# A two-layer attention and token-MLP kernel: odd columns of w2 packed and kept in DRAM, and fill work placed anew

## The chip, the core and the metric

The kernel runs on one core of a Trainium2 chip, in one launch. The metric is the device time of that launch in microseconds (us); the median of three runs before the change is 1305.59 us (1304.1 to 1305.82). All weights and activations are bf16 in DRAM; products accumulate in fp32 in PSUM.

## The reference, cut to what matters

`x` is 2048 positions by 1024 features. Two layers follow each other with the same weights:

```python
x = x + A(layernorm(x), wqkv, wo)      # attention over 8 positions at distance 2, 32 heads of 32
x = x + B(layernorm(x), w1, b1, w2, b2)
x = x + A(...)
x = x + B(...)

# A: q, k, v = x @ wqkv; position s attends to s, s-2, ..., s-14; then @ wo
# B mixes positions, not features (2048 positions -> 3584 -> 2048 positions):
h = layernorm(x)
u = gelu(einsum("bsd,sf->bdf", h, w1) + b1)
y = einsum("bdf,fs->bds", u, w2) + b2       # transposed back to positions x features
```

Because attention goes in steps of two, even positions never see odd ones inside A. In B all positions mix.

## The kernel before, in words

**Classes.** The positions are split by parity into class 0 (even) and class 1 (odd), 1024 positions each, in eight tiles of 128 positions. Attention runs class by class. In the MLP, a tile of output positions of class c needs every other column of w2: columns `c::2` of a block of 256 (`DIL` is 2).

**Stages of a layer.**

1. Attention (`Attn.stream`). TensorE projects q, k and v (L410). VectorE multiplies q with shifted k (L442), and TensorE adds those products up to scores with a selection matrix (L447). Softmax follows on VectorE and ScalarE (L453 to L468). The probabilities go to DRAM and come back spread over partitions (`pd`, `pb`, on POOL's queue), and VectorE multiplies and adds them with v (L503 to L509). Each class has two groups `n` of heads, so `n` runs from 0 to 3.
2. Output projection of a class (`out_proj`, L629). VectorE empties the PSUM banks and adds the residual (L650 or L653), the row goes to DRAM (`xa`), and a layernorm gives `h2`.
3. First MLP product (`gemm1`, L680), over 14 blocks `fb` of 256 columns of w1. For blocks below `NPART` the two classes are done apart: class 0's partial product is copied to `g` (L686), and later class 1's is added to it (L691) and goes through gelu (L692). For the others both classes accumulate in one bank, and gelu reads it (L688).
4. Second MLP product (`gemm2_tile`, L704), tile by tile: 28 blocks of w2 rows times two halves of the features. VectorE adds bias and residual (L709), the row goes to DRAM (`xb`), and in layer 0 a layernorm and a DMA transpose (L234) give the input `hT` of the next layer's attention.

**What runs inside what.** VectorE's attention work leaves TensorE idle, so other work is woven in as fill. `weave` takes a lead (attention and then class 1's output projection) and named fills, and keeps two clocks of its own, `pe` and `dve`, moved on by costs written beside each piece. When a lead piece must wait until some time, `reach` pulls fill pieces until `pe` is there. The fills are `second` (in layer 0 class 1's normalization; in layer 1 class 1's second MLP product of layer 0, the "class-1 pass"), `v_ahead` (class 1's v), `out0` (class 0's output projection), `partials` (class 0's first MLP product, blocks 0 to 5) and `late` (blocks 6 to `NPART`, whose `g` buffers hold class 1's v until attention is past them). Beside that, `weave` pulls a piece of `out0` each time lead work of `OUT0_GAP` has gone by on VectorE. Class 1's output projection begins with three row tiles at once, six banks without their last two contraction steps; the planner places it by `("less", "oT", -6.0)`, that is, 6 us by its own clock after the last attention piece.

After the weave come the blocks from `NPART` on for both classes, then blocks 0 to `NPART` for class 1, and then the second MLP product. In layer 0 only class 0's half of it runs here (the "class-0 pass"); the class-1 pass is woven into layer 1's attention. In layer 1 both classes run here, from the same w2 tiles. The order of instructions on each engine is then settled by the framework's scheduler.

**Queues and buffers.** SP's queue issues, in order, all loads of weights and rows and the transposes. POOL's issues stores and the probabilities. `wbp` is a pool of five slots for w1, w2, wo and v-weight tiles; a load waits on SP until TensorE is done with a slot, and what stands behind it on SP waits too. `w2_tiles` loads a block of 256 columns in four tiles of seven row blocks. `x2p` has four slots for rows (`xr`), normalized rows (`hb`) and `tmp`. `psp` has six PSUM banks. `tpl` has two slots, tag `T`, used by attention.

Of the kernel before, what the change touches and what calls it, by code (L numbers as in the profile page):

```python
# [13 lines left out]
BF16 = mybir.dt.bfloat16  # L14

P = 128
# [3 lines left out]
DIL = 2  # L20
# [6 lines left out]
def kernel(  # L27
# [32 lines left out]
    FB = 256  # L60
    NFB = F // FB
    GF = FB // P
    NPART = 10
    NW2 = 4
    HF = FT // NW2
    SLACK = 0.5
    PB_LAG = 12.0
    PDW = 4 * SB * W * TB + 512
    OUT0_GAP = 7.0
    assert D == H * DH and W == 8 and SC == 1024 and HD * KD == H and SB * CH == 32  # L70
    scale = float(DH) ** -0.5

# [97 lines left out]

    xa = [[dram.tile([SC, D], BF16, name=f"xa{li}{c}") for c in range(DIL)] for li in range(2)]
    xb = [dram.tile([SC, D], BF16, name=f"xb{c}") for c in range(DIL)]
    pd = [dram.tile([CH, PDW], BF16, name=f"pd{n}") for n in range(2 * DIL * NCQ)]

    xin_v = x_in.rearrange("(i m c) d -> c i m d", m=P, c=DIL)
# [433 lines left out]
    def out_proj(at_, c, res, dst, h2, on_act):  # L609

        early = 0 if on_act else 3
        if early:
            yield "pe", 1.28 * early * NDC, [("oT", 0), ("less", "oT", -6.0)], [], 0.0
        dst_v = rows(dst)
        wo_t = [[None, None] for _ in range(NDC)]
        for n in range(NDC):
            for hf in range(2):
                wt = wb("wo", [P, KD // 2, 512])
                nc.sync.dma_start(out=wt[:], in_=wo_v[hf, :, :, n * 512:(n + 1) * 512])
                wo_t[n][hf] = wt  # L620
        for hf in range(2):
            h2[c][hf] = hx(f"h2{c}{hf}", [P, NT // 2, D])
        banks = {}

        def multiply(i, n, kts):
            if (i, n) not in banks:
                banks[(i, n)] = bank()
            for kt in kts:
                nc.tensor.matmul(banks[(i, n)][:], lhsT=at_.oT[c][kt][:, i * P:(i + 1) * P],  # L629
                                 rhs=wo_t[n][kt // 4][:, kt % 4, :], start=(kt == 0), stop=(kt == KD - 1))  # L630

        def kts(i):
            return range(KD - 2 if i < early else 0, KD)

        for i in range(early):
            for n in range(NDC):
                multiply(i, n, range(KD - 2))
        xrs = Rows([res[i] for i in range(NT)], 2)
        for i in range(NT):
            if early:  # L640
                yield "pe", 0.43 * len(kts(i)), ["oT"], [], 3.6
                on_act = i % 2 == 0
            xn = xrs.take()
            s1 = st("s1", [P, NDC]) if on_act else None
            for n in range(NDC):
                cols = slice(n * 512, (n + 1) * 512)
                multiply(i, n, kts(i))
                ps = banks.pop((i, n))
                if on_act:
                    nc.vector.scalar_tensor_tensor(out=xn[:, cols], in0=ps[:], scalar=1.0, in1=xn[:, cols], op0=ALU.mult,  # L650
                                                   op1=ALU.add, accum_out=s1[:, n:n + 1])
                else:
                    nc.vector.tensor_tensor(out=xn[:, cols], in0=ps[:], in1=xn[:, cols], op=ALU.add)  # L653
            nc.gpsimd.dma_start(out=dst_v[i], in_=xn[:])
            h = h2[c][i // 4][:, i % 4, :]
            if on_act:
                nm, rs = stats_act(xn[:], 1.0 + EPS, eps2, h, s1)
                norm_act(h, xn[:], nm, rs)
            else:
                mean, rs = stats_dve(xn[:], 1.0 + EPS, eps2)  # L660
                norm_dve(h, xn[:], mean, rs)
            if not early:
                yield 3.5, 0.0
# [31 lines left out]
    def gemm2_tile(c, i, w2t, xs, dst, hT, on_act=False, end=False):  # L695
        xo = xs.take()
        halves = [slice(n * 512, (n + 1) * 512) for n in range(NDC)]
        groups = [halves[:1], [slice(512, 768)], [slice(768, 1024)]] if end else [halves]
        for cols in groups:
            acc = [bank() for _ in cols]  # L700
            for n in range(NW2):
                for ft in range(n * HF, (n + 1) * HF):
                    for ps, xc in zip(acc, cols):
                        nc.tensor.matmul(ps[:, 0:xc.stop - xc.start], lhsT=w2t[n][:, ft % HF, c::DIL],  # L704
                                         rhs=g[ft // GF][:, ft % GF, xc], start=(ft == 0), stop=(ft == FT - 1))
                if n < NW2 - 1:
                    yield 1.5 * len(cols), 0.0
            for ps, xc in zip(acc, cols):
                nc.vector.scalar_tensor_tensor(out=xo[:, xc], in0=ps[:, 0:xc.stop - xc.start], scalar=b2_sb[:, i, c:c + 1],  # L709
                                               in1=xo[:, xc], op0=ALU.add, op1=ALU.add)  # L710
            yield 1.5 * len(cols), 0.75 * len(cols)
            if end:
                nc.sync.dma_start(out=dst[:, cols[0]], in_=xo[:, cols[0]])
        if not end:
            nc.gpsimd.dma_start(out=dst, in_=xo[:])
        if hT is None:
            return
        hb = x2("hb")
        if on_act:
            nm, rs = stats_act(xo[:], 1.0, eps1, hb[:])  # L720
            norm_act(hb[:], xo[:], nm, rs)
        else:
            mean, rs = stats_dve(xo[:], 1.0, eps1)
            norm_dve(hb[:], xo[:], mean, rs)
        to_hT(hb[:], hT, c, i)
        yield 0.0, 0.0 if on_act else 2.0

    def w2_tiles(i):
        tiles = []
        for n in range(NW2):  # L730
            t = wb("w2", [P, HF, FB])
            nc.sync.dma_start(out=t[:], in_=w2_v[:, n * HF:(n + 1) * HF, i * FB:(i + 1) * FB])
            tiles.append(t)
        return tiles

    def run(*its):
        for _ in chain(*its):
            pass

    def weave(lead, fills, lags):  # L740
# [35 lines left out]
        for kind, *unit in lead:  # L776
            if kind == "open":
                after = {"out0": "oT", "partials": "out0", "late": "out0", "v_ahead": "second"}.get(unit[0])
                opened[unit[0]] = when.get(after, float("inf")) if after else pe
            elif kind == "drain":  # L780
                while unit[0] in opened:
                    pull(True)
            elif kind == "at":
                pe, dve = unit
            elif kind == "pe":
                cost, waits, sets, then = unit
                reach(ready(pe, waits))
                pe += cost
                when.update((x, pe + 2.0) for x in sets)
                if then:  # L790
                    dve = max(dve, pe) + then
            else:
                cost, waits, sets, lag, then = unit
                dve = ready(dve, waits) + cost
                if then:
                    reach(dve)
                    pe += then
                when.update((x, dve + lag) for x in sets)
                if list(opened)[:1] == ["out0"] and opened["out0"] < pe:
                    due += cost  # L800
                    if due > OUT0_GAP:
                        due -= OUT0_GAP
                        pull()
        while pull(True):
# [4 lines left out]
    for li in range(2):  # L809
# [22 lines left out]
        def second_class():  # L832
            new_hT(hT, 1)
            xs = Rows([rows(xa[0][1])[i] for i in range(NT)], 1)
            for i in range(NT):
                if first:
                    prologue_tile(1, i, hT)
                    yield 0.0, 2.0 * (i % 2 == 0)
                else:
                    yield from gemm2_tile(1, i, w2_tiles(i), xs, xb[1][i * P:(i + 1) * P, :], hT, on_act=i < NT - 2)  # L840

        def v_ahead():
            if not first:
# [18 lines left out]
        if first:  # L862
            with at(top):
                ln_exp_table()
            hT = [[None, None] for _ in range(DIL)]
            new_hT(hT, 0)
            xs = Rows([rows(xa[0][0])[i] for i in range(NT)], 1)
            for i in range(NT):
                run(gemm2_tile(0, i, w2_tiles(i), xs, xb[0][i * P:(i + 1) * P, :], hT))
        else:  # L870
            xs = Rows([rows(xa[1][c])[i] for i in range(NT) for c in range(DIL)], 1)
            for i in range(NT):
                w2t = w2_tiles(i)
                for c in range(DIL):
                    run(gemm2_tile(c, i, w2t, xs, out_v[c, i], None, end=(i == NT - 1 and c == DIL - 1)))
# [30 lines left out]
```

## Time and profile before

| | before |
|---|---|
| median of three runs | 1305.59 us |
| profiled execution, time | 1303.7 us |
| profiled execution, span | 1301.9 us |
| TensorE busy | 1274.3 us (98%) |
| VectorE busy | 669.5 us (51%) |
| ScalarE busy | 463.9 us (36%) |
| mean granted TensorE clock | 0.997 |
| DMA moved | 173.00 MB, mean 133 GB/s |

The span is the time from the first to the last instruction of the profiled execution. In a line of a timeline the columns are start, duration, engine, source line, operation, and what is written from what; in brackets stands the idle time before it and what ended that. In a line of waits they are the waiting instruction, what released it, the total, how often, and the longest.

Where the stages lie in the span, by TensorE's timeline: layer 0's attention and fills up to 288.8 us, class 1's output projection to 323.5, first MLP product to 464.5, class-0 pass to 561.2; layer 1's attention, with the class-1 pass from 575 to 758.7, then fills up to 925.5, output projection to 953.3, first MLP product to 1105, second to the end.

### The profile page before, as it was taken

Reading aid. Unit: us, or ns where it says so; the run is one execution under the profiler, and the core shown is the slowest. Engines: PE = TensorE matmul, PEld = TensorE weight load, DVE = VectorE, ACT = ScalarE, POOL = GpSimd, SP = SyncE. Lnnn points to the kernel's source line nnn. Section 1 sums busy time; section 2 is a strip of 40 time slices with the busy share of each in tenths; the row PEclk is TensorE's granted clock in tenths of the full one; section 3 lists DMA queues with packets and bytes.
Section 4 is the critical chain, followed back from the end, with each engine's and each line's share of the span. In section 5 each row is a group of like instructions: output and inputs, shape, how many; then the busy total and the mean of one; then the engine's idle time right before and its main releaser. Section 6 shows DMA issues by size and latency. Waiting matters only on the chain. (4 is left out here: it accounts for less than half of the span.)

```text
span 1301.9 us, 15529 instructions
## 1 busy us (share of the span) xinstructions
PE 1274.3 (98%) x6284; PEld 575.2 (44%) x6284; DVE 669.5 (51%) x845; ACT 463.9 (36%) x788; POOL 60.8 (5%) x166
## 2 busy tenths in 40 slices
PE   8999999998999999999999999999999999999999
PEld 4344444443444444444444444444444444444444
DVE  6879899988003423335896734879920044011011
ACT  6845447634313410024414535475352244000000
POOL 3000001001000000000000000010000000000000
PEclk9999999998999999999999999999999999999999
DMA  9843436653422268753659772338252321434331
GB/s 257 181 121 97 106 105 170 172 136 107 135 66 81 75 156 225 213 144 109 165 160 239 188 203 65 90 122 226 81 172 62 92 81 57 135 112 131 113 112 53
DMA packets 243544, 173.00 MB, mean 133 GB/s; under 512 B 32208, under 2 KB 227152, under 8 KB 241424
## 3 DMA queue, kind: packets, MB, share of 16 engines
q1 hardware_dynamic: 233648, 133.45, 38.1%
q0 software_dynamic: 9248, 37.51, 10.2%
q8 instruction: 49, 0.80, 0.3%
q10 hardware_dynamic: 576, 1.05, 0.2%
q14 instruction: 23, 0.19, 0.0%
HBM read 146.81 MB, written 18.87 MB: 127 GB/s over the span
## 5 line engine op out<-in xcount | busy, mean ns | idle before, releaser
L704 PE MATMUL ps<-g,w 128*128 128x512 bf16 (+1 forms) x1820 | 390.7, 376 | 3.4 <-ACT v L417 2.2
L680 PE MATMUL ps<-h,w 128*128 128x512 bf16 x1792 | 388.9, 379 | 4.3 <-ACT h L231 3.0
L704 PEld LDWEIGHTS <-w 128*128 128x128 bf16 x1820 | 177.4, 98 | 215.0 <-issue 6.9
L680 PEld LDWEIGHTS <-w 128*128 128x128 bf16 x1792 | 175.0, 98 | 217.4 <-issue 6.0
L410 PE MATMUL ps<-hT,wq 128*128 128x512 bf16 (+1 forms) x1112 | 243.4, 375 | 3.5 <-DVE xr L709 2.2
L691 DVE TENSOR_TENSOR tmp<-ps,g 128x512 f32<-128x512 f32 x80 | 55.4, 692 | 232.8 <-PE ps L680 232.8
L709 DVE SCALAR_TENSOR_TENSOR xr<-ps,b_sb,xr 128x512 bf16<-128x512 f32 (+1 forms) x65 | 45.6, 737 | 251.7 <-PE ps L704 211.8
L442 DVE TENSOR_TENSOR T<-q,k 128x4096 bf16<-128x4096 bf16 x60 | 135.5, 2285 | 63.5 <-ACT q L414 52.9
L410 PEld LDWEIGHTS <-wq 128*128 128x128 bf16 x1112 | 108.4, 100 | 133.1 <-issue 15.0
L507 DVE TENSOR_TENSOR pr<-pr 128x2048 bf16<-128x2048 bf16 (+1 forms) x128 | 119.1, 945 | 0.2
L410 PE MATMUL ps<-hT,wv 128*128 128x512 bf16 x448 | 101.8, 380 | 0.0
L629 PE MATMUL ps<-wo,oT 128*128 128x512 bf16 x384 | 90.5, 382 | 1.6 <-DMA wo<-in_A_wo_dram 1.6
L417 ACT CAST k<-ps 128x1024 bf16<-128x1024 f32 x60 | 60.8, 1015 | 76.6 <-PE ps L410 74.6
L503 DVE TENSOR_TENSOR pr<-pb,v 128x2048 bf16<-128x2048 bf16 x64 | 76.0, 1215 | 23.2 <-DMA pb<-pd 13.5
L692 ACT ACTIVATE g<-tmp,b_sb 128x512 bf16<-128x512 f32 x80 | 57.7, 722 | 82.1 <-DVE tmp L691 82.1
L503 DVE TENSOR_TENSOR pr<-pb,g 128x2048 bf16<-128x2048 bf16 x64 | 76.2, 1212 | 9.0 <-DMA pb<-pd 9.0
L686 ACT CAST g<-ps 128x512 bf16<-128x512 f32 x80 | 45.8, 591 | 73.3 <-PE ps L680 73.3
L410 PEld LDWEIGHTS <-wv 128*128 128x128 bf16 x448 | 48.6, 112 | 50.5 <-issue 7.2
L629 PEld LDWEIGHTS <-oT 128*128 128x128 bf16 x384 | 37.4, 98 | 48.7 <-issue 5.1
L688 ACT ACTIVATE g<-ps,b_sb 128x512 bf16<-128x512 f32 x32 | 22.0, 687 | 83.2 <-PE ps L680 83.2
L414 ACT CAST q<-ps 128x512 bf16<-128x512 f32 x60 | 34.8, 584 | 46.7 <-PE ps L410 46.7
L417 ACT CAST g<-ps 128x1024 bf16<-128x1024 f32 x36 | 36.6, 1017 | 40.6 <-PE ps L410 40.6
(90 smaller groups left out, 597.6 us busy)
## 6 DMA issues: line engine op xcount, KB each, us to landing
w<-in_B_w_dram SPq DMA_DIRECT2D x96, 448.0 KB, 3.7
w<-in_B_w_dram SPq DMA_DIRECT2D x56, 512.0 KB, 4.5
wq<-in_A_wqkv_dram SPq DMA_DIRECT2D x38, 512.0 KB, 4.2
pb<-pd POOLq DMA_DIRECT2D x16, 1024.0 KB, 10.1
wo<-in_A_wo_dram SPq DMA_DIRECT2D x16, 512.0 KB, 5.1
xa<-xr POOLq DMA_DIRECT2D x32, 256.0 KB, 3.3
xr<-xa SPq DMA_DIRECT2D x32, 256.0 KB, 3.6
wv<-in_A_wqkv_dram SPq DMA_DIRECT2D x14, 512.0 KB, 6.9
```

The source lines that it names most:

```text
L410: nc.tensor.matmul(ps[:, lo:hi], lhsT=cols, rhs=self.hT[c][hf][:, kt, lo:hi], start=(kt == 0), stop=(kt == KD - 1))
L417: nc.scalar.copy(out=window(buf, 0, PADK + hf * HT, [(KW + 1, 2), (1, HT)]), in_=ps[:].unsqueeze(1).to_broadcast([P, 2, HT]))
L442: nc.vector.tensor_tensor(out=T[:], in0=q.unsqueeze(1).to_broadcast([P, 4, SC]), in1=window(k, par, 2, [(2, 4), (1, SC)]), op=ALU.mult)
L503: nc.vector.tensor_tensor(out=pr[:, :, u, :], in0=pb[:, :, u, :], in1=window(self.v_of(c, dt), par, 2 + hf * HT, [(TB, 4), (2, 4), (1, TB) ...
L507: nc.vector.tensor_tensor(out=pr[:, :, 0:wd, :], in0=pr[:, :, 0:wd, :], in1=pr[:, :, wd:2 * wd, :], op=ALU.add)
L629: nc.tensor.matmul(banks[(i, n)][:], lhsT=at_.oT[c][kt][:, i * P:(i + 1) * P], rhs=wo_t[n][kt // 4][:, kt % 4, :], start=(kt == 0), stop=( ...
L680: nc.tensor.matmul(ps[:], lhsT=wt[c][:, i, fl * P:(fl + 1) * P], rhs=h2[c][i // 4][:, i % 4, dc * 512:(dc + 1) * 512], start=(k == 0), sto ...
L686: nc.scalar.copy(out=gs, in_=ps[:])
L691: nc.vector.tensor_tensor(out=tmp[:], in0=ps[:], in1=gs, op=ALU.add)
L692: nc.scalar.activation(out=gs, in_=tmp[:], func=ACT.Gelu_apprx_tanh, bias=b1_sb[:, ft:ft + 1])
L704: nc.tensor.matmul(ps[:, 0:xc.stop - xc.start], lhsT=w2t[n][:, ft % HF, c::DIL], rhs=g[ft // GF][:, ft % GF, xc], start=(ft == 0), stop=(f ...
L709: nc.vector.scalar_tensor_tensor(out=xo[:, xc], in0=ps[:, 0:xc.stop - xc.start], scalar=b2_sb[:, i, c:c + 1], in1=xo[:, xc], op0=ALU.add, ...
```

## The change

In the class-0 pass, ScalarE now copies the odd columns of each w2 tile into a packed tile `odd`, and its own DMA queue stores that to a DRAM buffer `w2_odd`. The class-1 pass in layer 1 reads `w2_odd` in two tiles per block instead of w2 in four; the matmuls read them unstrided. `gemm2_tile` gets a function for its weights. Three numbers of the fill planning change: `NPART` from 10 to 12 (14 blocks in all), the start of class 1's output projection from 6 to 12 us after the last attention piece, and pieces of `out0` that `OUT0_GAP` calls for are pulled only while `pe < dve + AHEAD`.

```diff
-    NPART = 10
+    NPART = 12
...
     OUT0_GAP = 7.0
+    AHEAD = 10.0
...
+    w2_odd = [dram.tile([P, F], BF16, name=f"w2o{i}") for i in range(NT)]
...
         if early:
-            yield "pe", 1.28 * early * NDC, [("oT", 0), ("less", "oT", -6.0)], [], 0.0
+            yield "pe", 1.28 * early * NDC, [("oT", 0), ("less", "oT", -12.0)], [], 0.0
...
-                        nc.tensor.matmul(ps[:, 0:xc.stop - xc.start], lhsT=w2t[n][:, ft % HF, c::DIL],
+                        nc.tensor.matmul(ps[:, 0:xc.stop - xc.start], lhsT=w2t(ft, c),
...
-    def w2_tiles(i):
+    def w2_tiles(i, keep=False):
         tiles = []
+        odd = tpl.tile([P, NW2, HF, P], BF16, name="odd", tag="T") if keep else None
         for n in range(NW2):
             t = wb("w2", [P, HF, FB])
             nc.sync.dma_start(out=t[:], in_=w2_v[:, n * HF:(n + 1) * HF, i * FB:(i + 1) * FB])
+            if keep:
+                nc.scalar.copy(out=odd[:, n], in_=t[:, :, 1::DIL])
             tiles.append(t)
-        return tiles
+        if keep:
+            nc.scalar.dma_start(out=w2_odd[i].rearrange("p (f m) -> p f m", m=P), in_=odd[:].rearrange("p n f m -> p (n f) m"))
+        return lambda ft, c: tiles[ft // HF][:, ft % HF, c::DIL]
+
+    def w2_kept(i):
+        tiles = []
+        for n in range(2):
+            t = wb("w2", [P, FT // 2, P])
+            nc.sync.dma_start(out=t[:].rearrange("p f m -> p (f m)"), in_=w2_odd[i][:, n * F // 2:(n + 1) * F // 2])
+            tiles.append(t)
+        return lambda ft, c: tiles[ft // (FT // 2)][:, ft % (FT // 2), :]
...
-                    if due > OUT0_GAP:
+                    if due > OUT0_GAP and pe < dve + AHEAD:
...
-                    yield from gemm2_tile(1, i, w2_tiles(i), xs, xb[1][i * P:(i + 1) * P, :], hT, on_act=i < NT - 2)
+                    yield from gemm2_tile(1, i, w2_kept(i), xs, xb[1][i * P:(i + 1) * P, :], hT, on_act=i < NT - 2)
...
-                run(gemm2_tile(0, i, w2_tiles(i), xs, xb[0][i * P:(i + 1) * P, :], hT))
+                run(gemm2_tile(0, i, w2_tiles(i, keep=True), xs, xb[0][i * P:(i + 1) * P, :], hT))
```

## The prediction, on record before the result

> **What bounds the kernel now.** I read parts 1 and 2 of the page, then TensorE's waits, then the timelines of TensorE and VectorE around the longest wait, then windows over the stage that gets new DMA work.
>
> ```profile
> PE 1274.3 (98%) x6284; PEld 575.2 (44%) x6284; DVE 669.5 (51%) x845; ACT 463.9 (36%) x788; POOL 60.8 (5%) x166
> PEclk9999999998999999999999999999999999999999
> ```
>
> TensorE is busy for 1274.3 of 1301.9 us. In the built order both kernels have equally many matmuls of the same shapes, and weight loads run beside them (44%), so reading packed instead of strided weights saves nothing by itself. To be won are TensorE's 27.6 idle us and the one dip of its clock, in the tenth slice (about 300 us). The largest of its waits is there:
>
> ```profile
> PE ps L629 <- DVE xr L650: 4.7, 1, 4.7
> ```
>
> TensorE's timeline at that place, and at the same code in the second layer:
>
> ```profile
> 296.17 3.19 PE L629 MATMUL ps<-wo,oT 128*128 128x512 bf16 x14
> 304.03 1.87 PE L629 MATMUL ps<-wo,v 128*128 128x512 bf16 x4 [4.67 <-DVE xr L650]
> ...
> 323.50 1.89 PE L680 MATMUL ps<-h,w 128*128 128x512 bf16 x8
> 326.35 18.95 PE L680 MATMUL ps<-h,w 128*128 128x512 bf16 x87 [0.96 <-DMA w<-in_B_w_dram]
> ...
> 932.79 3.19 PE L629 MATMUL ps<-wo,oT 128*128 128x512 bf16 x14
> 935.98 1.02 PE L629 MATMUL ps<-wo,v 128*128 128x512 bf16 x4
> ```
>
> VectorE's first evictions (L650) in the same two places:
>
> ```profile
> 303.28 0.69 DVE L650 SCALAR_TENSOR_TENSOR xr<-ps,xr 128x512 bf16<-128x512 f32 x1
> ...
> 935.24 0.69 DVE L650 SCALAR_TENSOR_TENSOR xr<-ps,xr 128x512 bf16<-128x512 f32 x1
> ```
>
> Class 1's output projection (L629, 128 matmuls) can fill six PSUM banks, 48 matmuls, before VectorE must empty one, and VectorE first finishes the last attention values. In layer 0 TensorE starts at 288.83, has its banks full at 299.4 and stands until 304.03. In layer 1 it starts at 925.45, only 9.8 us before L650, and does not stand. Four matmuls take 1.87 us behind the gap, 1.02 at full clock. The block takes 323.50 - 288.83 = 34.67 us in layer 0 and 953.25 - 925.45 = 27.80 in layer 1: the gap with its dip costs 6.87 us, 4.67 idle and 2.2 at half clock.
>
> **The change, part by part.**
>
> *"Less oT" at -12, layer 0.* The planner puts 24 more class-0 partial products (L680) ahead of that projection, 272 instead of 248 in the built order. At 0.216 us (80 take 17.3 us in layer 1) they are 5.2 us. The projection starts at 294.0, 9.3 us before L650 as in layer 1; the banks are full at 304.4, the first is free at 303.9. Gap and dip go: -6.9. Late next is its fourth wo load: it now waits for a w1 slot that is read until 16 matmuls before the projection and is needed 27 matmuls (5.8 us) later; the four wo loads there land in 4.8 us (median). 0, at worst +0.5.
>
> *The w1 load behind it.* At 326.35 TensorE waits 0.96 us for a tile whose slot comes free 20 matmuls (4.3 us) before its use. With 16 left-over partial matmuls instead of 8 this becomes 28 (6.0 us): -0.96. In layer 1 the projection is now followed by 8 left-over matmuls instead of a whole tile of 32, and the tile behind them stands at just those 20: +0.96. Together 0.
>
> *NPART 12.* Per layer two column blocks more are done class by class: in all 16 more copies (L686, 0.591 us), 16 more adds (L691, 0.692), and 16 activations at 0.722 (L692) instead of 0.687 (L688). TensorE needs 1.73 us for each such unit of eight matmuls, and VectorE idles 232.8 us in all before L691: 0. Uncovered, the adds would be 11 us. SP's w1 loads keep number and size.
>
> *AHEAD.* In layer 1, 16 of class 0's projection matmuls now follow a group of scores (L447) instead of leading it, and VectorE makes one product (L442, 2.29 us) in the pauses of 1.03 us between its evictions, not behind them all. I put its last eviction of that block (888.35) at 1.6 us earlier. TensorE waits for what follows from such evictions at 884.6 (0.47 us), 887.8 (0.34) and last here:
>
> ```profile
> 893.08 32.54 PE L680 MATMUL ps<-h,w 128*128 128x512 bf16 x150 [1.76 <-ACT h L231]
> ```
>
> Bounds 0 and -2.6 (all three); I take -1.3.
>
> *Class-1 pass, layer 1.* 32 loads of 448 KB in 512-byte pieces become 16 loads of as many bytes with 3,584 bytes in a row, and SP's queue is 16 issues shorter (0.37 us each). A slot of five now serves 28 matmuls instead of 14, so loads run further ahead. This wait goes, -1.1, since its load stood behind a transpose in SP's queue:
>
> ```profile
> 752.45 6.22 PE L704 MATMUL ps<-g,w 128*128 128x512 bf16 x28 [1.12 <-DMA w<-in_B_w_dram]
> ```
>
> The other waits of that pass (4.4 us from 681 to 722) follow VectorE's attention work and the queue on POOL behind its 1 MB pb loads; the diff touches neither: 0, with -2 to +1 for loads that shift. The 0.66 us at 765.6 end with the last transpose and stay.
>
> *Class-0 pass, layer 0: the price.* ScalarE gets 32 copies of 896 elements. Nearest are its SBUF operations, 628 ns for 512 (L213) and 1240 for 1024 (L231): about 1.1 us each. The every-other-element read is shown nowhere; I keep 0.9 to 2.2. With eight DMA issues (four on its queue took 4.15 us at the start) that is 5 to 11 us of each tile's 12.1, where it has 0.5 us of work. The new waits: a copy waits for its w2 load, and one stands between ln and rs (L193, L194). Queued behind it are rs, VectorE's norm, SP's transpose and, behind that in SP's queue, two w2 loads. A load of 3.9 us (median there) and the copy put rs some 2 us later, 4 if a write is in its way. The w2 load behind the transpose has about 12 us from slot to use, and lands in 3.9 when issued 2 to 4 us late: some 4 us remain. A w2 slot now also waits for its copy, which is done before TensorE reads the tile. 0 from ScalarE. The gelus of layer 0's last blocks also stand behind copies, by up to 2.4 us; four tmp buffers and six banks of 1.73 us each take that.
>
> The DMA engines are the open question. Columns: TensorE, weight loads, VectorE, ScalarE, POOL, clock, DMA share, GB/s.
>
> ```profile
> 476.60:488.70 12.10, 12.10 (x58) 5.49 (x57) 3.41 (x7) 0.50 (x2) 0.54 (x1) 1.00 0.95 198
> 512.90:525.00 12.10, 12.10 (x58) 5.50 (x57) 3.37 (x7) 0.50 (x2) 0.54 (x1) 1.00 0.78 217
> ```
>
> Per tile come 128 rows of 7,168 bytes, eight per engine. Packets of 4,096 bytes (the xb stores) take 165 ns (median), so a row takes 0.29 us and a tile's write 2.3 us, a share of 0.19: 0.78 becomes 0.97. By occupancy the stage sits at its limit, and any excess is TensorE's loss. The Trainium skill (Perfetto Trace Analysis, "Identifying the Most-Contended Engine") says to judge DMA by HBM utilization, since occupancy of 16 engines misleads. By that, 217 GB/s plus 0.917 MB in 12.1 us (76) is 293 GB/s, under the 358 it gives in "DMA: Bandwidth & Descriptors", Specifications, and under slices of 340 and more in this trace: 0 us. Against the change speaks that page's "Rules for kernel authors": a second issuing queue adds no bandwidth; ScalarE's writes share the engines with the w2 loads. So by occupancy 0 to +4 us, by utilization 0. I take 0, because five slots hold 12 us of slack[...]; +4 stays in the range.
>
> **The sum.** -6.9 + 0 + 0 - 1.3 - 1.1 + 0 = -9.3 us. The profiled execution took 1303.7 us (span 1301.9), which gives 1294.4. The median of the runs, 1305.59, lies 1.9 above it: 1305.6 - 9.3 = 1296.3.
>
> **Rivals.**
>
> *The writes cost part of it.* Windows at 0.95 and 0.90 before anything is added speak for it, no DMA wait of TensorE from 465 to 561 against. With +4: 1300.3. Likewise if only the clock dip went and half the gap stayed.
>
> *The gap does not go.* If VectorE's attention work moves with TensorE's (it reads nothing that TensorE delays there, which speaks against), only -2.4 remain: 1303.2, at the edge of no change.
>
> *The class-0 pass becomes DMA-bound: slower.* The pb loads' 8,192-byte packets take 565 ns on average, 14.5 GB/s per engine. At that rate a row of 7,168 takes 0.49 us, a tile's write 4.0 us, a share of 0.33; 0.80 + 0.33 = 1.13 of 12.1 us is 1.5 us per tile and 12.4 over eight: 1308.7. It decides once a write takes more than about 2.6 us per tile, and outweighs the gains above 3.6. The stores' 165 ns speak against.
>
> **How the numbers follow.** About 0.2%, 2.6 us, is what a measurement of this kernel can tell from no change: faster is below 1303.0, slower above 1308.2. My forecast 0.70 (1292 to 1299), part lost 0.15 (1300), gap stays 0.08 (1303, halved between faster and same), DMA-bound 0.07 (1308.7; 0.05 slower, 0.02 same). Faster 0.89, same 0.06, slower 0.05. The range of 1291.5 to 1302.5 takes in the forecast's bounds and the first rival.
>
> **What would show it.** Right: L629 in layer 0 without a wait on L650, the clock row at 9 throughout, no DMA wait near 750, a wait of about 1 us on w1 behind layer 1's projection, and TensorE without gaps in the w2_tiles stage at a DMA share above 0.9. Wrong: waits of L704 on w there, tiles longer than 12.1 us, or L629 still waiting for L650 with a dip of the clock.

## The result, and the profile after

The median went from 1304.96 us (1304.1 to 1305.82, four runs) to 1293.26 us (1291.79 to 1294.37, four runs): a ratio of 0.991, 95% interval 0.9892 to 0.9927. The profiled execution took 1291.79 us with a span of 1290.0, 11.9 less than before, where the sum had 9.3. The predicted 1296.3 us was 3.0 too high, and the range held the time.

The page after, in the same lines as before:

```profile
PE 1263.8 (98%) x6163; PEld 574.5 (45%) x6284; DVE 680.5 (53%) x861; ACT 502.7 (39%) x836; POOL 60.8 (5%) x166
PEclk9999999999999999999999999999999999999999
```

The clock row has no dip left. TensorE's shorter busy time is partly missing records (6163 of 6284) and partly the half-clock stretch that went. ScalarE carries 39 us more, and nothing waits long for it. In the list of TensorE's waits the first line shown of before, the one for L650, has no successor (L652 in the new numbering); the longest single wait is now 1.9 us:

```profile
PE sc L449 <- DVE T L444: 3.6, 3, 1.9
PE ps L631 <- DMA wo<-in_A_wo_dram: 2.4, 2, 1.7
PE ps L682 <- ACT h L233: 2.1, 3, 1.0
```

TensorE's timeline at class 1's output projection of layer 0 and behind it, and at the first tiles of w1 behind the projection of layer 1:

```profile
301.81 3.19 PE L631 MATMUL ps<-wo,oT 128*128 128x512 bf16 x14
304.83 1.03 PE L631 MATMUL ps<-wo,v 128*128 128x512 bf16 x3
...
322.10 8.15 PE L682 MATMUL ps<-h,w 128*128 128x512 bf16 x36
...
948.22 12.04 PE L682 MATMUL ps<-h,w 128*128 128x512 bf16 x54 [0.81 <-DMA w<-in_B_w_dram]
```

The block that stood for 4.67 us runs through, its first matmuls behind the old place of the gap take 1.03 us instead of 1.87, and it lasts 322.10 - 294.47 = 27.63 us. The wait for w1 has moved from layer 0 to layer 1. The class-0 pass, in the windows shown of before:

```profile
476.60:488.70 12.10, 12.05 (x56) 5.49 (x56) 3.36 (x6) 4.15 (x6) 0.54 (x1) 1.00 1.21 267
512.90:525.00 12.10, 12.05 (x57) 5.46 (x57) 3.43 (x7) 4.15 (x6) 0.54 (x1) 1.00 1.08 281
```

The DMA share is above 1 and no wait of TensorE shows: the pass takes 96.69 us before (464.49 to 561.18) and after (456.78 to 553.47).

### The profile page after: what moved, and what is told of

The parts are those of the page before. It is cut to its first block, busy times and chain, and to the rows that moved or that the text cites. A ratio compares the mean times of both kernels' runs of the same rounds, so it can differ in the third digit from the quotient of the medians.

```text
span 1290.0 us, 15498 instructions
## 1 busy us (share of the span) xinstructions
PE 1263.8 (98%) x6163; PEld 574.5 (45%) x6284; DVE 680.5 (53%) x861; ACT 502.7 (39%) x836; POOL 60.8 (5%) x166
## 5 line engine op out<-in xcount | busy, mean ns | idle before, releaser
L693 DVE TENSOR_TENSOR tmp<-ps,g 128x512 f32<-128x512 f32 x96 | 66.4, 692 | 211.3 <-PE ps L682 206.0
L694 ACT ACTIVATE g<-tmp,b_sb 128x512 bf16<-128x512 f32 x96 | 69.3, 721 | 93.3 <-DVE tmp L693 92.9
L688 ACT CAST g<-ps 128x512 bf16<-128x512 f32 x96 | 55.1, 589 | 91.5 <-PE ps L682 85.8
L737 ACT COPY odd<-w 128x896 bf16<-128x896 bf16 x32 | 30.0, 938 | 56.0 <-DMA w<-in_B_w_dram 55.8
```

The source lines that it names most:

```text
L688: nc.scalar.copy(out=gs, in_=ps[:])
L693: nc.vector.tensor_tensor(out=tmp[:], in0=ps[:], in1=gs, op=ALU.add)
L694: nc.scalar.activation(out=gs, in_=tmp[:], func=ACT.Gelu_apprx_tanh, bias=b1_sb[:, ft:ft + 1])
```

## The experiments

Ratios are against the kernel before, run beside each on the same chip. Stage lengths are read from TensorE's timeline, from the start of one block to the start of the next.

### Each part alone

Four kernels change one thing in the kernel before. First, the output projection's start:

```diff
-            yield "pe", 1.28 * early * NDC, [("oT", 0), ("less", "oT", -6.0)], [], 0.0
+            yield "pe", 1.28 * early * NDC, [("oT", 0), ("less", "oT", -12.0)], [], 0.0
```

> The kernel before with one number changed: "less oT" at -12 instead of -6. Theory A (cover): layer 0's output projection starts 5.2 us later, its 4.67 us wait for L650 and the half-clock stretch go, and the block takes 27.6 instead of 34.7 us: about -6.9 us, in layer 1 a wait of about 0.9 us for w1 behind the projection in exchange for the 0.96 in layer 0, so -7 in all. Rival (the wait moves with TensorE): the wait stays near 4.7 us, no change within 1 us.

Measured: 1298.52 us, ratio 0.9943 (0.9928 to 0.9958). Layer 0's projection takes 27.63 us without a wait, and a wait for w1 of 0.86 us stands behind that of layer 1. The gap and the exchange of w1 waits belong to this one edit.

Second, the class-0 pass with its copies and stores, while the class-1 pass still reads w2 (the stored `w2_odd` is not used):

```diff
-                run(gemm2_tile(0, i, w2_tiles(i), xs, xb[0][i * P:(i + 1) * P, :], hT))
+                run(gemm2_tile(0, i, w2_tiles(i, keep=True), xs, xb[0][i * P:(i + 1) * P, :], hT))
```

> The kernel before with ScalarE's copies and the stores to w2_odd in the class-0 pass; the class-1 pass still reads w2, so w2_odd is written and not used. Theory A: the class-0 pass takes 96.7 us as before, time unchanged within 1 us, although the DMA share of that stage is then above 1.0. Rival (the DMA engines become the bound): tiles of 12.1 us grow to 12.5 or more, +3 to +12 us.

Measured: 1306.03 us, ratio 0.9994 (0.9985 to 1.0003); the class-0 pass takes 96.7 us. The price of packing and storing is nothing that can be measured.

Third, the same and in addition the kept half read in the class-1 pass, with the old planner numbers:

```diff
-                    yield from gemm2_tile(1, i, w2_tiles(i), xs, xb[1][i * P:(i + 1) * P, :], hT, on_act=i < NT - 2)
+                    yield from gemm2_tile(1, i, w2_kept(i), xs, xb[1][i * P:(i + 1) * P, :], hT, on_act=i < NT - 2)
```

> The kernel before with the stores and with the class-1 pass reading w2_odd; none of the planner's numbers changed. Theory A as predicted: only the 1.1 us wait for w2 near 750 goes, -1.1 us. Theory B (from the trace after: less DMA work beside the probabilities' round trip through DRAM lets POOL's queue land sooner): -3 to -3.5 us, with the waits of L704 for ACT v near 698 and of L410 for L709 near 715 gone. Rival: 0, the gain of that pass belongs to the fill planning.

Measured: 1303.43 us, ratio 0.9984 (0.997 to 0.9998). The wait for w2 near the end of the pass is gone, and those for rows and v in the middle of it shrank: more than the one wait the prediction counted.

Fourth, the condition on `AHEAD`:

```diff
-                    if due > OUT0_GAP:
+                    if due > OUT0_GAP and pe < dve + AHEAD:
```

> The kernel before with AHEAD alone. Theory A: VectorE's product moves into the pauses of layer 1's class-0 output projection, TensorE's waits for h and L650 at 884 to 893 (2.6 us) shrink by 1.3 us. Rival: the waits only change place, 0.

Measured: 1306.72 us, ratio 1.0014 (1.0002 to 1.0027): no gain, if anything a loss. The stage from the end of the class-1 pass to layer 1's projection is 1.3 us shorter (165.65 instead of 166.94). But TensorE's timeline of this kernel shows the projection of layer 1 (L630 here) with the gap that only layer 0 had:

```profile
941.73 1.02 PE L630 MATMUL ps<-wo,v 128*128 128x512 bf16 x4 [2.23 <-DVE xr L651]
...
944.10 1.91 PE L630 MATMUL ps<-wo,v 128*128 128x512 bf16 x4
```

TensorE arrives sooner, VectorE does not, and the six banks are full before L651 empties one: 2.23 us of idling and a stretch at half clock. The block takes 31.87 us instead of 27.80: 1.3 us won, 4.1 lost, of which some 1.7 are the half clock. This profiled execution, at 1311.13 us, is one of the four slowest of twelve (the other eight took 1304.8 to 1307.3), so its net loss of 2.8 us is more than the 1.8 us of the median.

### AHEAD taken back out of the kernel after

```diff
-                    if due > OUT0_GAP and pe < dve + AHEAD:
+                    if due > OUT0_GAP:
```

> The kernel after without the condition on AHEAD, so that the exchange's fill in layer 1 is spread as in the kernel before. If AHEAD is worth in the kernel after what it took off the waits on h in the kernel before (1.3 us), this is 1.3 us slower than after, with no wait on VectorE and full clock in layer 1's projection (27.6 us), since the -12 covers it. If AHEAD only moves a wait, it is as fast as after within 0.3 us.

Measured: 1295.18 us, ratio 0.9916 (0.9903 to 0.993), 1.4 to 1.8 us slower than two kernels run beside it that keep the condition (1293.76 and 1293.34, below); the intervals of the ratios overlap, and its class-1 pass is also 1.7 us longer than that of the kernel after, so the median can't be put down to this step. The trace shows the step itself. The three waits behind class 0's projection are back as in the kernel before:

```profile
875.81 2.75 PE L682 MATMUL ps<-h,w 128*128 128x512 bf16 x12 [0.47 <-ACT h L233]
878.90 3.18 PE L682 MATMUL ps<-h,w 128*128 128x512 bf16 x14 [0.34 <-DVE xr L652]
883.84 0.38 PE L682 MATMUL ps<-h,w 128*128 128x512 bf16 x1 [1.76 <-ACT h L233]
```

They sum to 2.57 us. In the kernel after they are two, of 1.40 us:

```profile
873.13 6.85 PE L682 MATMUL ps<-h,w 128*128 128x512 bf16 x30 [1.04 <-ACT h L233]
880.34 3.83 PE L682 MATMUL ps<-h,w 128*128 128x512 bf16 x17 [0.36 <-ACT h L233]
```

With -12 in place the projection has no wait either way (27.63 us in both). So `AHEAD` pays 1.2 us, but only together with -12: the two edits are not additive. Its mechanism went as predicted: counted from the end of the class-1 pass, VectorE's last eviction of class 0's projection came 1.65 us earlier than before (128.19 instead of 129.84), where 1.6 was expected.

### The piece count alone

```diff
-    NPART = 10
+    NPART = 12
```

> The kernel before with NPART 12 instead of its old value and nothing else. If the pieces' number bears on nothing that TensorE waits for, it is the time of the kernel before within 0.5 us and all stage lengths agree within 0.2 us. If the finer pieces are part of the gain, it is 1 us or more faster, with shorter waits in the attention of layer 0 or layer 1.

Measured: 1306.26 us, ratio 1.0002 (0.999 to 1.0013), with every stage's length within 0.2 us of before except layer 0's attention, which is 2.8 us longer. Most of that is its first part, up to the first L629, which none of the edits reaches. It ends at 185.8 to 186.6 us in nine of the fourteen profiles and at 187.9 to 188.3 in five, this one among them: in these five, and in none of the nine, a wait of 2.04 to 2.05 us for VectorE at about 105 us was followed by half clock (last section). `NPART` is neutral.

### How early the projection must come

The kernel after with -9 in the place of -12:

```diff
-            yield "pe", 1.28 * early * NDC, [("oT", 0), ("less", "oT", -12.0)], [], 0.0
+            yield "pe", 1.28 * early * NDC, [("oT", 0), ("less", "oT", -9.0)], [], 0.0
```

> The changed kernel with "less oT" at -9: 16 instead of 24 more partial products ahead of the projection, 3.45 us of cover for the 4.67 us wait. The remaining wait in layer 0 is about 1.2 us. Theory A (the clock drops only behind a long wait): no half-clock stretch, so +1.2 us there and -0.8 in layer 1, where 16 left-over products hide the w1 load: +0.4 us in all. Rival (any wait at this place drops the clock): +2 us or more.

Measured: 1296.08 us, ratio 0.9917 (0.9891 to 0.9942). TensorE's timeline of layer 0's projection:

```profile
302.14 3.19 PE L631 MATMUL ps<-wo,oT 128*128 128x512 bf16 x14
306.82 1.02 PE L631 MATMUL ps<-wo,v 128*128 128x512 bf16 x4 [1.50 <-DVE xr L652]
```

Part of the gap is left, 1.50 us, without a dip; the block takes 29.40 us. The gap closes as fill goes in front of it, as the step said, and -9 is not enough. The wait for w1 behind layer 1's projection is gone, as expected. This profile has the half clock at 105 us too, so its time can't be held against the expected +0.4 us.

With -14 in layer 1, and -12 in layer 0:

```diff
+            yield "pe", 1.28 * early * NDC, [("oT", 0), ("less", "oT", -12.0 if at_.li == 0 else -14.0)], [], 0.0
```

> The kernel after, with 14 instead of 12 taken off the oT capacity in layer 1 (12 in layer 0 as before): 40 instead of 24 more matmuls of the MLP ahead of layer 1's projection than in the kernel before. If the wait on w1 behind layer 1's projection (0.81 us) is only a matter of how soon the MLP follows the load, it stays or moves, since the MLP's matmuls are taken from behind the projection: 0 to 0.8 us gained. If more fill in front of the projection has a price of its own, the wait of the attention's end on the projection shows as a later start of the layer's last MLP: 0 to 0.7 us lost. Expected -0.4 us, which the measurement hardly tells from nothing; the trace tells whether the 0.81 us is there.

Measured: 1293.34 us, ratio 0.9907 (0.989 to 0.9924). The 0.81 us behind layer 1's projection are gone, yet the time is that of the kernel after: a difference of this size does not show in the medians.

### What the stores would cost if there were more of them

The kernel after, storing each packed tile twice and three times to DRAM (the further copies are read by nobody; 358 GB/s in the expectations is the figure that the prediction took from the Trainium skill):

```diff
+            nc.scalar.dma_start(out=w2_more[0][i].rearrange("p (f m) -> p f m", m=P), in_=odd[:].rearrange("p n f m -> p (n f) m"))
```

> The changed kernel with each packed tile stored twice, the second time to a buffer that nobody reads: 7.3 MB more of writes in the class-0 pass. If the share of the 16 engines were the limit, that stage (share about 1.1 in the changed kernel) would go to 1.3 and lose about 20 us. By HBM utilization, 293 + 76 = 369 GB/s against a limit of 358, it would lose about 3 us. If five slots of prefetch and idle time between still cover it: 0.

> The changed kernel with each packed tile stored three times: 14.7 MB more of writes. By HBM utilization 445 GB/s would be asked for against 358: the class-0 pass of 96.7 us becomes 120, +23 us. By the engine share, 1.5 instead of 1.0: +48 us. If neither binds at these rates, 0.

Measured: 1308.42 us, ratio 1.0009 (0.9999 to 1.002), for two stores, and 1325.23 us, ratio 1.0133 (1.0096 to 1.017), for three. The class-0 pass takes 103.66 and 115.65 us. The windows over the whole pass, for before, after, two and three stores in this order (the last two columns are DMA share and GB/s):

```profile
464.50:561.20 96.70, 96.70 (x450) 43.83 (x449) 24.23 (x44) 5.49 (x16) 3.77 (x7) 1.00 0.81 212
```

```profile
456.80:553.50 96.70, 96.28 (x442) 43.83 (x449) 24.23 (x44) 31.04 (x44) 3.78 (x7) 1.00 1.05 277
```

```profile
459.40:563.00 103.60, 98.85 (x449) 43.96 (x448) 24.20 (x43) 31.31 (x44) 3.78 (x7) 0.98 1.09 312
```

```profile
459.40:575.00 115.60, 101.79 (x449) 44.46 (x448) 24.19 (x43) 31.29 (x44) 3.78 (x7) 0.96 1.09 334
```

The share goes from 0.81 to 1.05 at no cost, and from 1.05 to 1.09 at 7 and at 19 us: it does not say what room is left. The mean rate does put the four in order, 277 GB/s free and 312 not, but no rate shows as a limit. The kernel after has 12 us stretches at 313 to 318 GB/s without a wait, and with three stores the 4 us in which a wait of 3.12 us ends have a lower rate and a higher share than the 4 us behind them:

```profile
506.00:510.00 4.00, 2.02 (x10) 0.95 (x11) 0.00 (x0) 1.44 (x3) 0.00 (x0) 1.00 1.21 294
510.00:514.00 4.00, 4.00 (x20) 1.79 (x19) 3.36 (x6) 2.69 (x3) 0.54 (x1) 1.00 1.14 367
```

What grows is the time from issue to landing of a w2 load, 3.9 us before, 5.4 after, 7.4 and 8.2 with two and three stores (medians in this pass), until TensorE waits for them. With two stores and with three:

```profile
PE ps L707 <- DMA w<-in_B_w_dram: 4.8, 3, 2.1
PE ps L707 <- DMA w<-in_B_w_dram: 13.8, 5, 4.0
```

Most of the rest of the 7 and 19 us is half clock behind these waits (a mean clock of 0.98 and 0.96). The order that the prediction feared has a part in it: with two stores, the tile that TensorE waits for at 546.23 was issued behind a transpose (534.44), which stood behind `rs` (533.63), which stood behind a copy that had waited 7.79 us for a w2 load of its own. How much is slower loads alone and how much this order was not separated. So the rival "the added stores make the class-0 pass slower" was real, but from the second store of 0.92 MB per tile on; the first pays nothing. Two stores also delay the transpose at the pass's end, and the attention behind it loses another 7.6 us.

### Why the class-1 pass gained more than one wait

The region of layer 1's attention that holds the class-1 pass (608.46 to 758.51 before, 600.73 to 747.41 after) became 3.4 us shorter, where the prediction had 1.1. SP's queue at the pass's first tile, before and after:

```profile
659.16 22.17 SPq L732 DMA_DIRECT2D w<-in_B_w_dram  x8
681.38 0.55 SPq L606 DMA_DIRECT2D xr<-xa  x1
```

```profile
651.42 19.13 SPq L747 DMA_DIRECT2D w<-w2o  x4
670.59 0.46 SPq L608 DMA_DIRECT2D xr<-xa  x1
```

The residual's strip (xr) stands behind the loads, and with twice the work per slot the last of them gets its slot 3 us earlier, the time of 14 matmuls. SP is then done with them sooner. In the same trace ScalarE's layernorm, whose row waits for the xb store on POOL's queue, waited 5.49 us instead of 7.64. Rivals: that the traffic is lighter because the pieces are long, or because SP issues fewer transfers. Two kernels separate them. Both read the kept half in 224 KB transfers, as many as the kernel before issues; the first into slots of its own,

```diff
-        for n in range(2):
-            t = wb("w2", [P, FT // 2, P])
-            nc.sync.dma_start(out=t[:].rearrange("p f m -> p (f m)"), in_=w2_odd[i][:, n * F // 2:(n + 1) * F // 2])
+        for n in range(NW2):
+            t = wb("w2", [P, HF, P])
+            nc.sync.dma_start(out=t[:].rearrange("p f m -> p (f m)"), in_=w2_odd[i][:, n * F // NW2:(n + 1) * F // NW2])
```

> The changed kernel with w2_odd read in four tiles of 224 KB per block instead of two of 448 KB: the bytes of the changed kernel, the number and order of SP's issues and the slot turns of the kernel before; every other engine has the same instructions in the same order as in the changed kernel. Theory B (fewer bytes beside POOL's round trip): as fast as the changed kernel within 1 us. Rival (deeper prefetch and a shorter SP queue): the class-1 pass loses the 3.4 us that it gained.

the second by pairs into one slot, so that the slots turn over as in the kernel after:

```diff
-            nc.sync.dma_start(out=t[:].rearrange("p f m -> p (f m)"), in_=w2_odd[i][:, n * F // 2:(n + 1) * F // 2])
+            for m in (2 * n, 2 * n + 1):
+                nc.sync.dma_start(out=t[:, (m % 2) * HF:(m % 2 + 1) * HF].rearrange("p f m -> p (f m)"),
+                                  in_=w2_odd[i][:, m * F // NW2:(m + 1) * F // NW2])
```

> The kernel after, with each kept half of the class-1 pass brought into its slot by two transfers of 224 KB instead of one of 448 KB: the same bytes, the same turns of the slots and the same orders on every engine as after; what differs is that SyncE issues 32 transfers instead of 16. If the loads finish early because a slot is turned over half as often (so that the residual's strip and the partial sums behind them land sooner), layer 1's attention with the class-1 pass takes 146.7 us as after, the waits of 0.65 and 1.33 us stay away, the strip is issued about 19 us after the pass's first load, and the time is that of the kernel after, within 0.5 us. If it is the size of the transfers or the number that SyncE issues, it looks like the run with four separate tiles: 148.9 us, both waits back, the strip about 22 us after, and 2.2 us slower than after.

Measured: 1294.92 us, ratio 0.9911 (0.9884 to 0.9938), for four tiles, and 1293.76 us, ratio 0.9904 (0.9888 to 0.992), for pairs. The times do not tell them apart; the traces do. SP's queue with four tiles, and with pairs:

```profile
651.34 22.13 SPq L747 DMA_DIRECT2D w<-w2o  x8
673.52 0.43 SPq L608 DMA_DIRECT2D xr<-xa  x1
```

```profile
652.74 19.81 SPq L748 DMA_DIRECT2D w<-w2o  x8
672.66 0.40 SPq L608 DMA_DIRECT2D xr<-xa  x1
```

and ScalarE's first layernorm behind it, in the kernel after, then with four tiles, then with pairs:

```profile
686.69 0.63 ACT L215 ACTIVATE hb<-xr 128x512 bf16<-128x512 bf16 x1 [5.49 <-DMA xb<-xr]
688.73 0.63 ACT L215 ACTIVATE hb<-xr 128x512 bf16<-128x512 bf16 x1 [7.64 <-DMA xb<-xr]
687.45 0.63 ACT L215 ACTIVATE hb<-xr 128x512 bf16<-128x512 bf16 x1 [4.92 <-DMA xb<-xr]
```

With four tiles the 22 us and the 7.64 us of before are back, with packed weights; with pairs they are away, with as many issues. So neither the bytes per piece nor the number of issues makes the 3 us on SP: the turns of the slots do. TensorE's way from the pass's long run (652.33 in the kernel after) to the end of the pass is 98.5 us before, 97.4 with four tiles, 94.5 with pairs and 95.1 after.

All runs together: the six kernels with 22 us there took 97.4 to 98.8 us (98.3 on average), the eight with 19 to 20 us 94.5 to 96.8 (95.4). The spread shows that the early strip is not all of it: the kernel with `AHEAD` taken out has SP's queue of the kernel after, and yet its layernorm waited 7.25 us for the xb store and a wait of TensorE of 1.32 us was back; with three stores that wait is there as well. That the turns of the slots put the strip 3 us earlier is shown; how its place shortens the transfers on POOL's queue, and with them TensorE's waits, is argued and not shown.

## Why the prediction was right, point by point

| step | predicted, us | measured, us |
|---|---|---|
| start of layer 0's projection, without the fill added | 0 | +0.5 |
| its gap and the dip of the clock | -6.9 | -7.0 |
| w1 wait, layer 0 | -1.0 | -1.0 |
| class-0 pass | 0 | 0.0 |
| class-1 pass and its region | -1.1 | -3.4 |
| AHEAD, and the stage up to layer 1's projection | -1.3 | -1.6 |
| w1 wait, layer 1 | +1.0 | +0.8 |
| sum | -9.3 | -11.7 |

The profiled executions differ by 11.9 us; 0.2 us are not assigned to a step.

- **The gap.** The step held in each of its numbers: 24 matmuls (5.2 us) in front, no wait on VectorE, and the idle time and the half clock together. The fourth wo load, named as late next, was not late. The +0.5 us are at waits of layer 0's attention, mostly for an earlier wo tile (1.08 us before, 1.71 after), which over the runs lies between 1.1 and 2.4 us with no order by edit. One reading was loose: -12 was said to bring the start to 9.3 us before L650 "as in layer 1", where it is 9.8. The difference did no harm, but it shows how little room there is: in layer 1 of the kernel before, the first bank came free at 935.85 and TensorE was back at 935.98.
- **The exchange of w1 waits.** It came as counted from the distance between a slot's last reader and the load's first. One goes and the other comes, so it sums to about nothing.
- **AHEAD.** The size was right (1.2 us on the waits for h; the rest of the 1.6 is 0.4 us at the last transpose's wait, which the prediction let stay and which lies between 0.3 and 0.8 us over the runs), but the prediction treated it as independent of -12. Alone it gains nothing, as its kernel showed, because it uses up the 0.1 us by which layer 1's projection cleared VectorE. That the step came out all the same was luck: -12 covers the projection in layer 1 too, and the prediction counted that cover for layer 0 alone.
- **The class-1 pass, the mis-sized step.** Of the waits from 681 to 722 the prediction said that the diff touches neither VectorE's attention work nor POOL's queue, and put 0 with -2 to +1, so the -3.4 lies just beyond its margin. The wait near 752 went as said, but it went with four tiles too, where a slot still serves 14 matmuls, so the slot's larger load was not what it needed. The other waits and what lies between them shrank by 2.2 us on average over the runs (97.6 us without the wait for w2 in the six kernels, 95.4 in the eight) where the slots turn over half as often and SP reaches the strip 2 to 3 us earlier. The prediction read that SP's queue would be shorter and loads run further ahead, and did not follow what stands behind them in SP's queue.
- **The rivals.** "The writes cost part" fell with the stores alone; "the gap does not go" with the -12 alone; of "the class-0 pass becomes DMA-bound: slower", the loss is real from the second store on, and whether the DMA engines' rate alone makes it stays open.

**The class-0 pass.** A copy takes 0.94 us, at the cheap end of the 0.9 to 2.2 kept and below the 1.1 worked out: if reading every other element has a price, it does not show beside that estimate. In the groups of the page (count, then total and mean, then the idle time before):

```profile
L737 ACT COPY odd<-w 128x896 bf16<-128x896 bf16 x32 | 30.0, 938 | 56.0 <-DMA w<-in_B_w_dram 55.8
```

ScalarE idles 56 us before the copies, waiting for w2 tiles, and nothing on the path minds. A row of 7,168 bytes took 297 ns on average, 272 at the median, where 0.29 us was worked out. The two rules parted here: by occupancy the excess of 0.05 to 0.21 over a full share would have cost TensorE 0.6 to 2.5 us in such a tile, by the utilization rule of the Trainium skill (Perfetto Trace Analysis, "Identifying the Most-Contended Engine") nothing. Nothing was lost, so taking 0 rather than the +4 end was right. But the 358 GB/s of "DMA: Bandwidth & Descriptors", Specifications, that the prediction set against its estimate of 293 is no limit that these runs show: 277 were measured, and with three stores 358 over the 12 us from 506 on and 413 over the last 4 of them. What the runs bear out is the other reason given for the 0, the slack of the five slots: loads that landed in 5.4 us instead of 3.9 were still in time.

The parts do not add: alone the -12 gives -0.57%, the kept half -0.16%, `AHEAD` +0.14% and `NPART` nothing, together -0.6%, while the kernel after has -0.9%. That is 4 us, give or take another 4 by the intervals (an estimate). `AHEAD` would be 3 of them: +1.8 alone by its median, -1.2 beside the -12 by the traces.

## What to carry to other kernels

Where an engine with full banks waits for another, count both distances: how far the start must move, and what the moved fill leaves behind it; and treat any edit that makes the first engine earlier as one that uses up that distance. When a pool's tiles become fewer and longer-lived, follow the queue that issues the loads to the next transfer behind them, since that is what moves. Judge room for added DMA traffic neither by the busy share of the DMA engines nor by a figure in GB/s alone, but by how long the loads take from issue to landing against the time until they are needed, and find where it ends by adding more traffic than the change does.

## What the runs showed of the hardware that was not expected

- **A DMA share above 1.** The summed busy time of packets exceeds 16 engines' time (1.05 over the whole class-0 pass, 1.21 in slices) with no wait anywhere, and stands at 1.09 when the rate goes from 312 to 334 GB/s: the busy share is likely to hold time in which packets wait, though no run separated that.
- **The clock after a wait.** The length of TensorE's wait alone does not decide whether its clock drops. With three stores it dropped behind a wait of 1.98 us and not behind one of 3.12; the same wait of 2.04 to 2.05 us at 105 us was followed by half clock in five profiles and not in five others. What parts them is where the wait falls in time. Within a profile the changes of the clock lie a whole number of steps of 3.413 us apart (with three stores it drops at 192.76, 523.85, 554.57 and 585.29 us, 97, 9 and 9 steps). Cut along these steps, the stretches around the two waits are (columns as before; the first of each pair holds the wait or most of it):

```profile
189.35:192.76 3.41, 1.43 (x8) 0.58 (x6) 3.41 (x5) 0.00 (x0) 0.62 (x1) 1.00 0.92 256
192.76:196.17 3.41, 3.41 (x10) 1.18 (x8) 3.41 (x8) 0.78 (x3) 1.05 (x3) 0.50 0.13 51
503.37:506.78 3.41, 1.50 (x7) 0.49 (x5) 0.00 (x0) 0.00 (x0) 0.00 (x0) 1.00 1.20 246
506.79:510.20 3.41, 2.21 (x11) 1.03 (x12) 0.18 (x1) 1.44 (x3) 0.00 (x0) 1.00 1.22 291
```

TensorE is busy for 1.43 us (42%) of the first and for 1.50 us (44%) of the third; the longer wait is shared out over two stretches. So it is in all fourteen profiles: each of the 17 stretches at full clock in which TensorE was busy for 42% or less was followed by one at half clock, and none of the 5246 with 43% or more. A single wait then has to take about 1.95 us of one stretch (estimate: 57% of 3.413), and from about 3.9 us on it does so wherever it falls: the eight waits from 4.01 to 5.24 us all dropped the clock, and none of 1.94 us or less did. A dropped stretch costs up to 1.7 us, half its length; before, the gap of 4.67 us dropped two.
